# Keeping the whole triangle of a forward substitution in two PSUM banks, in a recurrence-and-experts kernel

## The chip, the cores and the metric

One Trainium2 core runs the kernel. The engines named here are TensorE (PE; its weight loads are PEld), VectorE (DVE), ScalarE (ACT), GpSimd (POOL) and SyncE (SP, which issues most transfers). The metric is the device time of one execution in microseconds (us), as the median over runs.

## What is computed

A recurrence with a 40x40 state over 768 steps, for 4 batches and 8 heads, followed by a layer of 8 experts. Cut to what matters:

```python
for t in range(S):                                   # S = 768, state [4,8,40,40]
    y[:, :, t] = einsum('bhd,bhde->bhe', rt, state)
    Sa = einsum('bhde,bhe->bhd', state, at)
    state = state*wt[:, :, None, :] - einsum('bhd,bhe->bhde', Sa, bt) \
            + einsum('bhd,bhe->bhde', vt, kt)
x = y.transpose(0, 2, 1, 3).reshape(B*S, H*D)        # 3072 tokens of 320
# for tokens whose x @ w_skip > 0: the expert of the largest gate logit,
out = xc + gate_w * (relu(xc @ w1[e]) @ w2[e])       # other tokens: out = x
```

## The kernel before

The 768 steps are cut into 24 chunks of 32 steps (`c`), four chunks to a phase (`ph`, `j` is the chunk in it). Inside a chunk the steps are coupled by a triangular 32x32 system per batch, head and chunk; its inverse is made ahead, for the four chunks of a phase at once. The chain from chunk to chunk is then matmuls alone: `rs` (state times r), `ux` (right-hand side), `uq` (times the inverse, read from `TB`), `sst` (new state), and `yy` (output, into `py`, multiplied by DVE into `XS`). Beside this chain each phase prepares the next one: scans of the decays on DVE (`scan_z`, `scan_w`), products on POOL (`kbm`, `l1a`, and the mask `R1t<-R1t,mc` behind each `uq`), the coupling matrices (`m1`: a PSUM tile that ACT copies and DVE transposes out), transposes (`kbt`, `wtt`), `m2`, and the routing of finished tokens (`route`: `xpose`, `score`, a rank `rk`).

The inverse itself is `tinv` (line 390): a forward substitution on DVE over the four chunks, 128 partitions wide. The coupling matrix `NLt` lies in SBUF (all tiles of that area appear as `M` in the trace). The triangle `X` is cut by columns. Columns 0 to 7 (`SPL=8`) lie in PSUM, in `X0`, which the trace calls `px`. Columns 8 to 31 lie in SBUF, in `Xi`. At step `i` group 0 handles row `j=i` of the PSUM part and group 1 row `j=i+8` of the SBUF part: a multiply of a column of `NLt` by a row of `X` into `tmp_`, and a subtraction of that from the rows below. Group 0 runs for 30 steps, group 1 for 22, so an inverse has 104 such instructions. In the trace group 0's are `M<-M,px` and `px<-px,M`; group 1's are both `M<-M`. At the end ACT copies `X0` into `Xi` (line 412) and DVE transposes the whole into `TB`. The first phase's inverse is made in another way (`tinv0`); `tinv` runs five times, for phases 1 to 5.

Eight PSUM banks of 512 floats are shared out at line 235: two `pq`, two `pc`, two `ps`, one `py` and one `px`. Chunks 0 and 1 and 22 and 23 are issued in the order in which the program is written, each ring of banks going round (`pq` serves `m1`, `kbt`, `wtt`, `m2` and routing). Chunks 2 to 21 are recorded and put in order by a planner (`Rec`, lines 58 to 210): it prices each instruction (line 93; a DVE `tensor_tensor` at 0.14 us + 1.05 ns per element, 1.6 times that slope where no operand is in PSUM), gives each PSUM tile a bank of `rec.banks` when its first instruction starts, whatever ring it was asked from, and keeps the two `ps` banks back for the state and for the oldest tile that waits. In its dependencies all `px` banks are one resource (line 90). What it emits is a fixed order for each engine. In the trace, L109 is what was issued directly and L209 what the planner emitted.

After the last chunk the banks are regrouped into three rings (line 767) for the experts (`experts`), whose matmuls end the kernel.

Of the kernel before, what the change touches and what calls it, by code (L numbers as in the profile page):

```python
# [8 lines left out]
F32 = mybir.dt.float32  # L9
I32 = mybir.dt.int32  # L10
AF = mybir.ActivationFunctionType
ALU = mybir.AluOpType
# [198 lines left out]
class Ring:  # L211
# [4 lines left out]
    def tile(s,shape,dt,tag=None,name=None):  # L216
# [4 lines left out]
        if len(shape)==2: return t  # L221
        ax=["abcd"[q] for q in range(len(shape)-1)]
        return t.rearrange("p ("+" ".join(ax)+") -> p "+" ".join(ax),**{a:v for a,v in zip(ax,shape[1:])})
G2=1; TD=(1,3); BU0=6; BU=(2,0,0,0); BX=(0,0,0,0,0,1,0,0,0,0,2,2,1,1,1,0,0,0,1,2,0,1,1,1,1,0,1,0,0); SPL=8; SCAN_POOL=0; RN=192; RB=((),()); RLAST=(('0c','1b','3a','3c'),('0a','0c')); P2=0
ROUTE=('0c',('0c','1b','3c'),('0c','1b','3c'))
WT=(1,0,0,0,1)
def attn(ctx,tc,i,m,out,X):
# [4 lines left out]
    cp=P("const",1).pool; wk=P("wk",1); wk2=P("wk2",2); wk3=P("wk3",3); wk4=P("wk4",4)  # L232
    pp=m.pp
    bk=lambda n,k: [pp.tile([128,512],F32,name=f"{n}{q}") for q in range(k)]
    PQ,PC,PS,PY,PX=bk("pq",2),bk("pc",2),bk("ps",2),bk("py",1),bk("px",1)
    rec.banks={t.name:t for t in PQ+PC+PS}; rec.rest=[t.name for t in PS]
    ps_c,ps_s,ps_p=(Ring(t,rec) for t in (PC,PS,PQ)); ps_y,ps_x=Ring(PY),Ring(PX); m.ps=ps_p
    V,A,G,TE,SP=nc.vector,nc.scalar,nc.gpsimd,nc.tensor,nc.sync
# [2 lines left out]
    NR1=2; NL=4; NL2=2; NTB=3  # L241
    mQ,idn=m.mQ,m.idn
    WR=m.WR
    mp=tc.tile_pool(name="M",bufs=1,side="right"); M=mp.__enter__().tile([128,13300],F32,name="M")
    off=[0]
    def mv(n):
        o=off[0]; off[0]+=n; return M[:,o:o+n]
    w_,Z_,rv,a_,AB_,NL_,X_,l3=(mv(n) for n in (1041,1042,1041,1024,1024,1024,1024,1024))
    AT_=[mv(256) for _ in range(2)]; Wx_=[mv(1040).rearrange("p (a b) -> p a b",a=16) for _ in range(4)]; tmp_=[mv(192) for _ in range(2)]; an=[0]
    sq=lambda t: t.rearrange("p (a b) -> p a b",a=32)  # L250
    KBa=[WR[:,2048*q:2048*q+2048].rearrange("p (u c q t) -> p u c q t",u=16,c=2,q=2) for q in range(4)]
    L1t=cp.tile([128,4096],F32,name="L1t")
# [80 lines left out]
    def m1(h,x,c,ev=None,late=None,FE=None):  # L333
# [11 lines left out]
        if c==0: an[0]+=1  # L345
        if c==0: AT[0]=AT_[an[0]%2].rearrange("p (h c t) -> p h c t",h=4,c=2) if h!=1 else SCR[:,1024+256*x:1280+256*x].rearrange("p (h c t) -> p h c t",h=4,c=2)
        at=AT[0]
# [42 lines left out]
    def tinv(ph):  # L390
        ab=AB[0]
        NLt=sq(NL_)
        V.transpose(NLt.rearrange("p a b -> p (a b)"),ab.rearrange("p a b -> p (a b)"))
        Xi=sq(X_)
        X0=ps_x.tile([128,32,SPL],F32)
        V.tensor_tensor(X0,NLt[:,0:SPL].rearrange("p s t -> p t s"),m.mT[:,:,0:SPL],ALU.mult)
        V.tensor_tensor(Xi[:,:,SPL:32],NLt[:,SPL:32].rearrange("p s t -> p t s"),m.mT[:,:,SPL:32],ALU.mult)
        V.memset(X0.rearrange("p a b -> p (a b)")[:,0:SPL*SPL:SPL+1],-1.0)
        V.memset(Xi.rearrange("p a b -> p (a b)")[:,33*SPL::33],-1.0)
        yield  # L400
        for i in range(1,31):
            q=[]
            for g,(j,lo,hi,X) in enumerate(((i,0,min(i,SPL),X0),(i+SPL,SPL,i+SPL,Xi))):
                if j>30: continue
                n=31-j; k=hi-lo
                tmp=tmp_[g]
                tv=tmp[:,:n*k].rearrange("p (a b) -> p a b",b=k)
                V.tensor_tensor(tv,NLt[:,j,j+1:32].unsqueeze(2).broadcast_to([128,n,k]),X[:,j,lo:hi].unsqueeze(1).broadcast_to([128,n,k]),ALU.mult)
                q.append((tv,X[:,j+1:32,lo:hi]))
            for tv,xv in q: V.tensor_tensor(xv,xv,tv,ALU.subtract)  # L410
            yield
        A.copy(Xi[:,:,0:SPL],X0)
        s0=(2*ph)%NTB; s1=(2*ph+1)%NTB
        t0=TBa[s0]; d=bass.AP(t0.tensor,t0.offset,(tuple(t0.ap[0]),(TBa[s1].offset-t0.offset,2),(32,16),(1,32)))
        V.transpose(d.rearrange("p h (x f) m -> p m x h f",x=2),Xi)
        yield
    def tinv0(Xi):
# [9 lines left out]
        for j in range(1,15):  # L427
            n=15-j; q=[]
            for g in range(G2):
                K=2//G2; k=slice(K*g,K*g+K)  # L430
                tv=tmp_[g][:,:K*n*j].rearrange("p (k a b) -> p k a b",k=K,b=j)
# [111 lines left out]
    def run_all(g):  # L543
        for _ in g: pass
    if 1:

        with tc.manual_schedule(engines={ET.Pool}):
# [4 lines left out]
            Xi=sq(X_)  # L552
# [46 lines left out]
            ps_p=Ring.of(pq.t+ps_y.t+ps_x.t)  # L599
# [20 lines left out]
            ps_p=r4  # L620
# [11 lines left out]
            ps_p=pq  # L632
# [17 lines left out]
        for c in range(NC):  # L650
            ph,j=divmod(c,4)
# [36 lines left out]
            if c==1: m1(3,1,0); m1(3,1,1); tg=tinv(1)  # L688
# [50 lines left out]
            if j==0 and c and ph+1<NPH: tg=tinv(ph+1)  # L739
# [24 lines left out]
        next(ra)  # L764
        yy(NC-1,1)
        run_all(ra)
        m.pr=[Ring.of(ps_c.t+ps_x.t),Ring.of(ps_s.t+ps_y.t),ps_p]
        p2=[m.pr[0].tile([128,512],F32) for _ in range(2)]; pt=[p2[0][:,0:256],p2[0][:,256:512],p2[1][:,0:256]]
        rb=m.route(xl[:,1:2],1,NC-1,lambda: onehot(1))
        warm(WT[1]); m.xacc(pt,0)  # L770
# [295 lines left out]
def build(tc,i,out):  # L1066
    with ExitStack() as ctx:
        cp=ctx.enter_context(tc.tile_pool(name="mcp",bufs=1))
        m=Moe(ctx,tc,i,out,cp)
        m.base1=cp.tile([128,8],F32,name="base1")  # L1070
        m.fi=cp.tile([1,3],I32,name="fi"); m.cw=cp.tile([128,24],F32,name="cw"); tc.nc.gpsimd.memset(m.cw,0.0)
        m.zc=cp.tile([128,1],F32,name="zc"); tc.nc.gpsimd.memset(m.zc,0.0)
        m.wc=cp.tile([128,1],F32,name="wc"); tc.nc.vector.memset(m.wc,-WMID)
        m.WR=cp.tile([128,11264],F32,name="WR"); m.raw=[m.WR[:,0:5632],m.WR[:,5632:11264]]
        P=lambda n,b,**k: tc.tile_pool(name=n,bufs=b,**k)
        with tc.manual_schedule(engines={ET.PE,ET.Activation,ET.DVE}), P("pp",1,space=PSUM) as m.pp, P("rt",1) as rt, P("xp",1) as xp:
            m.wk,m.xp=Static(rt,1),Static(xp,2)
            with ExitStack() as c2: attn(c2,tc,i,m,out,m.X)
            with P("mw2",2) as wk2, P("mw",1) as wk, P("mw4",4) as wk4: m.experts(wk,wk2,wk4,m.pr)
        general(m,m.fi,{q:i['raw_'+q] for q in 'rkvwab'},m.X)  # L1080
# [13 lines left out]
```

## Time and profile before

| what | value |
|---|---|
| median of 3 runs | 662.9 us (660.15 to 670.07) |
| the profiled execution's own time | 660.0 us |
| its span, first to last instruction | 658.2 us |
| mean granted TensorE clock | 0.88 |
| busy share of the span: PE, DVE, ACT, POOL | 77%, 79%, 64%, 49% |

The busy shares are means over stages with different limits. Three stages matter: the start and chunks 0 and 1 (to about 100 us), the planned chunks 2 to 21 (to about 480 us, in phases of some 80 us), and the last two chunks and the experts. How to read the rows below: "M<-M,px 128x120" is an instruction that writes a tile `M` of 128 partitions by 120 elements and reads `M` and `px`; "x44 | 26.7, 607 | 0.5" is 44 of them, 26.7 us busy in all, 607 ns each, and 0.5 us of idle time ahead of them.

### The profile page before, as it was taken

What the parts mean: (1) busy time and instruction counts of PE and PEld (TensorE: products, weight loads), DVE (VectorE), ACT (ScalarE), POOL (GpSimd) and SP (SyncE); (2) the same over time, 40 slices, a digit from 0 to 9 for tenths busy, and PEclk for the clock granted to TensorE, in tenths of its full rate; (3) what the DMA queues carried; (4) which work ended last, traced back from release to release, by engine and by line L of the source; (5) the groups of instructions that cost most, each with busy time, mean ns of one, the idle gap of its engine ahead of it and who ended that gap; (6) DMA issues with size and microseconds to landing.
All of it is one profiled execution on the core that took longest, in us unless ns stands there. A gap on an engine that the chain in (4) does not pass through costs nothing. (4 is left out here: it accounts for less than half of the span.)

```text
span 658.2 us, 30327 instructions
## 1 busy us (share of the span) xinstructions
PE 507.4 (77%) x13236; PEld 424.8 (65%) x13236; DVE 519.6 (79%) x1182; ACT 423.6 (64%) x1103; POOL 321.6 (49%) x256
## 2 busy tenths in 40 slices
PE   5766676687588778858758578888678799999994
PEld 2544465566476657637547466767566599899994
DVE  7998778988989789997998977884274458888871
ACT  6463565587766867757768578898966155455540
POOL 5491952645536665375733634333131156566661
PEclk9697778779877986888969799999977799999998
DMA  7784566352444525345334243454535166667200
GB/s 183 215 229 153 133 181 218 114 150 86 124 119 132 162 74 142 107 130 161 102 106 121 82 129 101 133 168 119 156 99 146 57 193 207 214 216 233 81 25 24
DMA packets 67817, 90.85 MB, mean 138 GB/s; under 512 B 32756, under 2 KB 54849, under 8 KB 66190
## 3 DMA queue, kind: packets, MB, share of 16 engines
q1 hardware_dynamic: 62638, 74.31, 39.0%
q0 software_dynamic: 5040, 14.54, 6.8%
q8 instruction: 106, 1.74, 1.1%
q14 instruction: 33, 0.27, 0.1%
HBM read 74.03 MB, written 17.08 MB: 138 GB/s over the span
## 5 line engine op out<-in xcount | busy, mean ns | idle before, releaser
L209 DVE TENSOR_TENSOR M<-M 128x130 f32<-128x130 f32 (+10 forms) x202 | 106.2, 526 | 2.2
L209 ACT COPY R1t<-pq 32x416 f32<-32x416 f32 (+4 forms) x218 | 84.1, 386 | 31.7 <-PE pq L209 28.7
L209 POOL TENSOR_TENSOR R1t<-R1t,mc 64x512 f32<-64x512 f32 x40 | 53.8, 1346 | 86.3 <-ACT R1t L209 62.8
L109 POOL TENSOR_TENSOR WL<-WR,WH 128x1280 fp32r<-128x1280 f32 (+1 forms) x21 | 57.6, 2779 | 8.7 <-ACT WH L109 8.6
L209 ACT COPY R1t<-pc 32x128 f32<-32x128 f32 (+4 forms) x146 | 53.3, 365 | 9.7 <-PE pc L209 7.7
L209 PE MATMUL py<-L2t,R1t 128*32 128x40 f32 x1280 | 22.9, 220 | 27.4 <-DVE XS L209 14.4
L209 POOL TENSOR_TENSOR WR<-WR,M 128x1024 f32<-128x1024 f32 x14 | 33.7, 2422 | 14.9 <-DMA WR<-kb 14.6
L109 ACT CAST WH<-WR 128x1024 fp32r<-128x1024 f32 (+1 forms) x35 | 39.6, 1132 | 0.0
L209 DVE TENSOR_TENSOR px<-px,M 128x168 f32<-128x168 f32 (+8 forms) x141 | 37.1, 263 | 3.1
L209 PEld LDWEIGHTS py<-L2t,R1t 128*32 128x32 f32 x1280 | 18.1, 124 | 31.9 <-issue 16.9
L109 DVE CAST ti<-xe 128x2 int32<-128x2 f32 x8 | 38.0, 4747 | 0.2
L109 POOL DMA_INDIRECT out<-ro,ti x16 | 15.7, 982 | 45.7 <-PE pq L109 21.8
L109 ACT ACTIVATE hH<-pc 128x512 fp32r<-128x512 f32 x21 | 12.6, 598 | 38.3 <-PE pc L109 38.3
L209 POOL DMA_INDIRECT xg<-XS,ix x20 | 24.6, 1232 | 25.1 <-DVE M L209 11.1
L209 DVE TENSOR_TENSOR M<-M,px 128x168 f32<-128x168 f32 (+8 forms) x141 | 34.7, 246 | 1.3
L209 DVE TENSOR_TENSOR_SCAN M<-M 128x1041 f32<-128x1041 f32 (+1 forms) x14 | 32.5, 2320 | 0.2
L209 POOL TENSOR_TENSOR M<-M,mc 128x256 f32<-128x256 f32 x16 | 12.1, 756 | 41.6 <-issue 25.4
L109 PE MATMUL pc<-xH,WH 128*128 128x256 f32 x126 | 32.4, 282 | 0.0
L109 DVE TENSOR_TENSOR WL<-WR,WH 128x1024 fp32r<-128x1024 f32 (+1 forms) x19 | 23.8, 1253 | 8.4 <-ACT WH L109 7.8
L209 DVE TENSOR_TENSOR R1t<-pc,D 40x512 f32<-40x512 f32 (+1 forms) x32 | 19.2, 601 | 13.3 <-PE pc L209 12.9
L209 PE MATMUL ps<-R1t,L2t 128*40 128x40 f32 (+1 forms) x512 | 26.3, 244 | 2.5 <-ACT R1t L209 1.1
L209 PE MATMUL pq<-UX,TB 32*32 32x72 f32 (+1 forms) x800 | 23.6, 262 | 5.5 <-ACT R1t L209 5.3
(380 smaller groups left out, 1692.9 us busy)
## 6 DMA issues: line engine op xcount, KB each, us to landing
WR<-kb SPq DMA_DIRECT2D x10, 1024.0 KB
WR<-w SPq DMA_DIRECT2D x16, 640.0 KB
WR<-w SPq DMA_DIRECT2D x16, 512.0 KB
vvt<-vv POOLq DMA_DIRECT2D x21, 256.0 KB, 4.1
rrt<-rr POOLq DMA_DIRECT2D x10, 512.0 KB, 5.6
M<-wt SPq DMA_DIRECT2D x9, 520.5 KB
M<-at SPq DMA_DIRECT2D x8, 512.0 KB
WR<-w SPq DMA_DIRECT2D x16, 256.0 KB
```

What stands on the lines that cost most here:

```text
L109: if not s.on: return fn(*a,**k)
L209: for fn,a,k,own in s.tasks[i].calls: fn(*[at(x,own) for x in a],**{n:at(x,own) for n,x in k.items()})
```

## The change

`X0` becomes 12 columns wide (`SPL=12`), and columns 12 to 31 go to a second PSUM tile `X1` of 20x20, which holds only the square that is not zero. To have a second `px` bank, one `pq` bank is given up. The planner then hands out five banks, and `pq` as a ring has one bank. Group 1 runs for 18 steps, so an inverse has 96 multiplies and subtractions. ACT copies two tiles into `Xi` at the end. The three rings of the experts keep their sizes, out of other banks.

```diff
-...; SPL=8; ...
+...; SPL=12; ...
-    PQ,PC,PS,PY,PX=bk("pq",2),bk("pc",2),bk("ps",2),bk("py",1),bk("px",1)
+    PQ,PC,PS,PY,PX=bk("pq",1),bk("pc",2),bk("ps",2),bk("py",1),bk("px",2)
-... M=mp.__enter__().tile([128,13300],F32,name="M")
+... M=mp.__enter__().tile([128,13400],F32,name="M")
-... tmp_=[mv(192) for _ in range(2)]; an=[0]
+... tmp_=[mv(240) for _ in range(2)]; an=[0]
-        Xi=sq(X_)
-        X0=ps_x.tile([128,32,SPL],F32)
+        Xi=sq(X_); K=32-SPL
+        X0=ps_x.tile([128,32,SPL],F32); X1=ps_x.tile([128,K,K],F32)
         V.tensor_tensor(X0,NLt[:,0:SPL].rearrange("p s t -> p t s"),m.mT[:,:,0:SPL],ALU.mult)
-        V.tensor_tensor(Xi[:,:,SPL:32],NLt[:,SPL:32].rearrange("p s t -> p t s"),m.mT[:,:,SPL:32],ALU.mult)
+        V.tensor_tensor(X1,NLt[:,SPL:32,SPL:32].rearrange("p s t -> p t s"),m.mT[:,SPL:32,SPL:32],ALU.mult)
         V.memset(X0.rearrange("p a b -> p (a b)")[:,0:SPL*SPL:SPL+1],-1.0)
-        V.memset(Xi.rearrange("p a b -> p (a b)")[:,33*SPL::33],-1.0)
+        V.memset(X1.rearrange("p a b -> p (a b)")[:,::K+1],-1.0)
         yield
         for i in range(1,31):
             q=[]
-            for g,(j,lo,hi,X) in enumerate(((i,0,min(i,SPL),X0),(i+SPL,SPL,i+SPL,Xi))):
+            for g,(j,o,X) in enumerate(((i,0,X0),(i+SPL,SPL,X1))):
                 if j>30: continue
-                n=31-j; k=hi-lo
-                tmp=tmp_[g]
-                tv=tmp[:,:n*k].rearrange("p (a b) -> p a b",b=k)
-                V.tensor_tensor(tv,NLt[:,j,j+1:32].unsqueeze(2).broadcast_to([128,n,k]),X[:,j,lo:hi].unsqueeze(1).broadcast_to([128,n,k]),ALU.mult)
-                q.append((tv,X[:,j+1:32,lo:hi]))
+                n=31-j; k=min(i,SPL) if g==0 else i
+                tv=tmp_[g][:,:n*k].rearrange("p (a b) -> p a b",b=k)
+                V.tensor_tensor(tv,NLt[:,j,j+1:32].unsqueeze(2).broadcast_to([128,n,k]),X[:,j-o,0:k].unsqueeze(1).broadcast_to([128,n,k]),ALU.mult)
+                q.append((tv,X[:,j+1-o:32-o,0:k]))
             for tv,xv in q: V.tensor_tensor(xv,xv,tv,ALU.subtract)
             yield
-        A.copy(Xi[:,:,0:SPL],X0)
+        A.copy(Xi[:,:,0:SPL],X0); A.copy(Xi[:,SPL:32,SPL:32],X1)
...
-        m.pr=[Ring.of(ps_c.t+ps_x.t),Ring.of(ps_s.t+ps_y.t),ps_p]
+        m.pr=[Ring.of(PC+PX[:1]),Ring.of(PS+PX[1:]),Ring.of(PQ+PY)]
```

## Rows read from the trace of the kernel before

**Rows 1.** The page's first part: busy us, share of the span, instructions of each engine.

```profile
PE 507.4 (77%) x13236; PEld 424.8 (65%) x13236; DVE 519.6 (79%) x1182; ACT 423.6 (64%) x1103; POOL 321.6 (49%) x256
```

**Rows 2.** Busy time by stretch: start:end, length, then engines, PEclk, DMA share, GB/s.

```profile
89.00:136.60 47.60, 33.16 (x1169) 28.02 (x1166) 41.77 (x132) 31.32 (x88) 19.47 (x17) 0.79 0.44 134
...
158.50:220.30 61.80, 46.01 (x1468) 37.71 (x1468) 57.84 (x153) 44.50 (x128) 31.84 (x27) 0.81 0.41 121
...
383.60:444.50 60.90, 50.73 (x1830) 41.34 (x1834) 47.64 (x174) 51.69 (x150) 19.06 (x20) 0.97 0.47 131
444.50:475.00 30.50, 25.11 (x890) 20.12 (x878) 11.02 (x35) 27.31 (x80) 8.09 (x8) 1.00 0.46 134
...
sum 247.00, PE 180.36 PEld 149.72 DVE 222.91 ACT 179.52 POOL 135.09; mean PE 60.12 PEld 49.91 DVE 74.31 ACT 59.84 POOL 45.03
```

**Rows 3.** Timeline of DVE: end of one inverse (TB), start of the next (M).

```profile
136.60 1.99 DVE L209 STREAM_TRANSPOSE TB<-M 128x1024 f32<-128x1024 f32 x1 [0.84 <-ACT M L209]
...
158.53 1.22 DVE L209 STREAM_TRANSPOSE M<-M 128x1024 f32<-128x1024 f32 x1
```

**Rows 4.** Groups of group-1 instructions, stretches from 89.0, from 136.6, from 383.6.

```profile
L209 DVE TENSOR_TENSOR M<-M 128x130 f32<-128x130 f32 (+10 forms) x26 | 10.0, 385 | 0.2
...
L209 DVE TENSOR_TENSOR M<-M 128x22 f32<-128x22 f32 (+10 forms) x44 | 26.7, 607 | 0.5
...
L209 DVE TENSOR_TENSOR M<-M 128x22 f32<-128x22 f32 (+10 forms) x44 | 14.4, 328 | 0.4
```

**Rows 5.** Instructions of tile px in the planned part: ns minimum/median/maximum, first and last start.

```profile
L209 DVE TENSOR_TENSOR M<-M,px x141: 131/240/345, 101.8 to 442.8; 128x168 f32<-128x168 f32 x9, 128x160 f32<-128x160 f32 x5, 128x152 f32<-128x152 f32 x5, 128x144 f32<-128x144 f32 x5
L209 DVE TENSOR_TENSOR px<-px,M x141: 161/267/357, 102.2 to 443.0; 128x168 f32<-128x168 f32 x9, 128x160 f32<-128x160 f32 x5, 128x152 f32<-128x152 f32 x5, 128x144 f32<-128x144 f32 x5
```

**Rows 6.** Timeline of POOL and DVE, 113 to 121 us: start, us, engine.

```profile
114.01 2.45 POOL L209 TENSOR_TENSOR R1t<-R1t,mc 64x512 f32<-64x512 f32 x1 [9.00 <-ACT R1t L209]
116.54 4.27 POOL L209 TENSOR_TENSOR WR<-WR,M 128x1024 f32<-128x1024 f32 x2
...
115.32 0.25 DVE L209 TENSOR_TENSOR M<-M,px 128x120 f32<-128x120 f32 x1
115.49 1.11 DVE L209 TENSOR_TENSOR M<-M 128x120 f32<-128x120 f32 x1
...
116.72 2.02 DVE L209 TENSOR_SCALAR D<-M 128x16 f32<-128x16 f32 x1
```

**Rows 7.** Groups with shapes kept apart: count, busy us, mean ns of one.

```profile
L209 DVE TENSOR_TENSOR M<-M,mc 128x768 f32<-128x768 f32 x4 | 6.0, 1498 | 0.0
...
L209 DVE TENSOR_TENSOR M<-M 128x130 f32<-128x130 f32 x20 | 5.8, 290 | 0.3
...
L209 DVE TENSOR_TENSOR px<-M,mc 128x256 f32<-128x256 f32 x4 | 3.3, 827 | 0.1
...
L209 DVE TENSOR_TENSOR px<-px,M 128x130 f32<-128x130 f32 x4 | 1.2, 301 | 0.1
...
L209 ACT COPY M<-px 128x256 f32<-128x256 f32 x5 | 1.9, 372 | 0.1
```

**Rows 8.** Timeline: a uq tile in its bank, filled by PE, emptied by ACT.

```profile
191.19 0.92 PE L209 MATMUL pq<-UX,TB 32*32 32x104 f32 x32
...
192.47 2.02 ACT L209 COPY R1t<-pq 32x416 f32<-32x416 f32 x4
```

**Rows 9.** Timeline, chunk 1: two m1 tiles in the two pq banks.

```profile
82.54 1.07 PE L109 MATMUL pq<-WR,L1t 128*32 128x64 f32 x64
...
83.24 0.88 ACT L109 COPY M<-pq 128x128 f32<-128x128 f32 x2
...
83.71 0.76 DVE L109 STREAM_TRANSPOSE M<-pq 128x128 f32<-128x128 f32 x2 [6.19 <-POOL WR L109]
```

**Rows 10.** Timeline, chunk 23: score behind m2, and the uq that follows.

```profile
495.71 0.62 PE L109 MATMUL pq<-wg,xT 128*32 128x9 f32 x24
495.88 1.06 ACT L109 COPY R1t<-pq 32x128 f32<-32x128 f32 x4
...
496.26 1.61 PE L109 MATMUL pc<-UX,TB 32*32 32x104 f32 x32
```

More of the change, by code (lines that the diff above doesn't have):

```diff
@@ L223, in tile @@
         return t.rearrange("p ("+" ".join(ax)+") -> p "+" ".join(ax),**{a:v for a,v in zip(ax,shape[1:])})
-G2=1; TD=(1,3); BU0=6; BU=(2,0,0,0); BX=(0,0,0,0,0,1,0,0,0,0,2,2,1,1,1,0,0,0,1,2,0,1,1,1,1,0,1,0,0); SPL=8; SCAN_POOL=0; RN=192; RB=((),()); RLAST=(('0c','1b','3a','3c'),('0a','0c')); P2=0
+G2=1; TD=(1,3); BU0=6; BU=(2,0,0,0); BX=(0,0,0,0,0,1,0,0,0,0,2,2,1,1,1,0,0,0,1,2,0,1,1,1,1,0,1,0,0); SPL=12; SCAN_POOL=0; RN=192; RB=((),()); RLAST=(('0c','1b','3a','3c'),('0a','0c')); P2=0
 ROUTE=('0c',('0c','1b','3c'),('0c','1b','3c'))
@@ L243, in attn @@
     WR=m.WR
-    mp=tc.tile_pool(name="M",bufs=1,side="right"); M=mp.__enter__().tile([128,13300],F32,name="M")
+    mp=tc.tile_pool(name="M",bufs=1,side="right"); M=mp.__enter__().tile([128,13400],F32,name="M")
     off=[0]
@@ L248, in attn @@
     w_,Z_,rv,a_,AB_,NL_,X_,l3=(mv(n) for n in (1041,1042,1041,1024,1024,1024,1024,1024))
-    AT_=[mv(256) for _ in range(2)]; Wx_=[mv(1040).rearrange("p (a b) -> p a b",a=16) for _ in range(4)]; tmp_=[mv(192) for _ in range(2)]; an=[0]
+    AT_=[mv(256) for _ in range(2)]; Wx_=[mv(1040).rearrange("p (a b) -> p a b",a=16) for _ in range(4)]; tmp_=[mv(240) for _ in range(2)]; an=[0]
     sq=lambda t: t.rearrange("p (a b) -> p a b",a=32)
```

## The prediction, made before the changed kernel was run

> **What bounds the kernel now.** I read the page's busy shares first, then the busy time by stretch, then the groups of instructions inside one stretch, then single stretches of the timeline. The shares of the whole span [rows 1] say little: DVE has 79%, PE 77%. So the planned part is cut at the transposes that finish an inverse into `TB`. There are five of them, the first at 136.6 us [rows 3], the others at 220.3, 300.6, 383.6 and 444.5 us, the bounds of my stretches. In the three full stages between 136.6 and 383.6 us (247.0 us together, 82.3 us each) DVE is busy 222.9 us, 90%; ACT has 59.8 us a stage (73%), PE 60.1 (73%) [rows 2]. Inside a stage, the stretch in which the inverse is made, from 158.5 us [rows 3] to its end, has DVE at 57.84 of 61.8 us, 94% [rows 2]. DVE sets the pace there. In the next stage, from 383.6 us, where nothing is prepared for a seventh phase, four chunks go through in 60.9 us with ACT at 51.69 us (85%) and DVE at 78%; after that comes a stretch with ACT at 27.31 of 30.5 us (90%) [rows 2]. So when DVE is not the limit, the chunk chain and ACT are, with ACT 85 to 90% busy.
>
> Now what DVE's time is made of. The 44 group-1 instructions of an inverse take 26.7 us in the first full stage, 607 ns each [rows 4]; the other two full stages look alike, within 2 us. The group-0 instructions, the same operation with one operand in PSUM, take 240 and 267 ns in the median and never more than 357 ns, in 282 of them [rows 5]. The sizes are alike: an inverse's group 1 has 2,024 products in 22 multiplies, 92 each, and its group 0 2,936 in 30, 98 each. So size does not explain 607 ns. The timeline does: while POOL works from 114.01 us on, a group-0 multiply takes 0.25 us as always, and the group-1 multiply of the same 120 elements right behind it takes 1.11 us and ends with the POOL instruction [rows 6]. Without POOL, group 1's largest forms average 290 ns [rows 7]. What an SBUF-only instruction pays is a wait for POOL, and it is paid on the engine that is the limit.
>
> **The change, part by part.** *Group 1 goes to PSUM.* I price it by the group-0 rows, 0.25 us each [rows 5]. The wait that goes is 44 x (0.607 - 0.25) = 15.7 us in a full stage, 26 x (0.385 - 0.25) = 3.5 us in the stretch from 89 us, and 44 x (0.328 - 0.25) = 3.4 us in the stage from 383.6 us [rows 4]. Eight instructions fewer take off 8 x 0.25 = 2 us. Against it, group 0 runs alone for 12 steps at the end and not 8, with each instruction waiting for the one before; other work of DVE can stand between them, so I book 1 us of the 2 us.
>
> [...] Group 1's 130-element form costs 290 ns in SBUF, and group 0's of the same size 301 ns [rows 7], so moving an instruction costs about 10 ns, 36 x 0.01 = 0.4 us an inverse. [...]
>
> *The start of an inverse.* Two multiplies, 256 elements into PSUM at 0.83 us and 768 at 1.50 us [rows 7], become 384 and 400 elements into PSUM. By the first row that is 2.5 us, by the second 1.5; against 2.3 us I count nothing.
>
> *The end.* ACT copies 384 and 400 elements in place of 256 at 0.37 us [rows 7]: at most 0.37 x 784/256 = 1.1 us, so +0.8 us for ACT, between the last subtraction and `TB`.
>
> *What a full stage then takes.* DVE needs 74.3 - 15.7 - 1 = 57.6 us. ACT needs 59.8 + 0.8 = 60.6 us, now the larger. At ACT's 85% a stage lasts 71.3 us; at 90% 67.7 us; if nothing followed DVE's gain, 82.3 us. I take 85%, because that stage has the same chain of four chunks. PE's 60.1 us is at a granted clock of about 0.8 (0.81 in the stretch from 158.5 us), and the stage that ran faster was granted 0.97 [rows 2], so PE is no earlier limit.
>
> *One bank less for the planner.* The program asks for 74 tiles in four chunks (4 `rs`, 8 `ux`, 8 `uq`, 8 `m1`, 8 `kbt`, 4 `wtt`, 8 `m2`, 10 of the routing, 16 `sst`). A `uq` tile is held from 191.19 to 194.49 us, 3.3 us [rows 8]. If all are held so long that is 244 us of bank time: 49% of six banks over 82.3 us, but 69% of five over 71.3 us. There is room, but bursts will wait. Lower bound nothing, since `m1` and `rs` tiles wait for DVE today and will be freed sooner; upper bound 16 us a stage, the whole gain. No row shows a plan with five banks; I take 2.7 us, in the lower part because the banks have room on average. A stage then lasts 74 us: 3 x (82.3 - 74) = 25 us gained. The planner also prices group 1 lower and takes both `px` banks as one resource; DVE is one queue, so I count nothing for either.
>
> *One `pq` bank where the order is written.* In chunk 1 thirteen tiles (`m1`, `kbt`, `wtt`, `m2`, one `s2`) go through `pq`. Now two `m1` are filled back to back, and both leave by 84.47 us [rows 9]. With one bank the second fill (half of 1.07 us) waits for the first transpose, and each pair ends about 1 us later. PE's queue stands meanwhile, with the chain behind it. Six pairs at 1 us give 6 us; PE is busy only 33.16 of 47.6 us there [rows 2], which hides some. Bounds 0 and 12 us, I take 3 us, which meets the 3.5 us that DVE gets back in the same stretch (88% busy, 3 us of it counted). In chunks 22 and 23 a `score` is filled at 495.71 us while `m2` is still being copied out until 496.94 us [rows 10]: it will wait 1.2 us, and the `uq` at 496.26 us is behind it on PE. A second such place follows from the code in chunk 22. I book 2 us, between 0 and 3. The stage from 383.6 us gets 0: ACT sets it, and what DVE gets back the banks take.
>
> **The sum.** 660.0 us (the profiled execution) - 25 - 3 + 3 + 0 + 2 = 637 us. That execution is 2.9 us under the median of the runs; I put the median at 638 us.
>
> **Rivals.** *A, all of it comes back:* no bank ever waits and ACT reaches 90%. A stage takes 67.7 us, 3 x 14.6 = 44 us, and 660 - 44 - 3 + 1 = 614 us. For it: the second stretch of 90% [rows 2], and a plan that was bound by DVE's waits, which it does not price. Against it: ACT has never been that busy over a whole stage.
>
> *B, the banks take the gain:* from 0.15 us of waiting per tile (74 x 0.15 = 11 us) a stage is back at 82 us, and the kernel at 660 to 665 us. For it: bank use goes from 49 to 69%, and more than half of it lies on three banks that every kind of tile may take. Against it: the order is planned for five banks.
>
> *C, slower:* the same wait, but on the chain. PE's queue is in order, so a `ux` that waits for a bank holds the `sst` behind it, and ACT's copies then come late, which hold the banks longer. From 15.4/74 = 0.21 us per tile the kernel is over 2% slower (11 us of gain and 13.3/3 us of loss in a stage); at 0.25 us a stage is 89.8 us and the kernel 684 us. Against it: today's holds have more than one tile's length of slack on average.
>
> *D, the waits move and do not go:* DVE still has instructions that wait for POOL, such as the `TENSOR_SCALAR` of 16 elements that took 2.02 us at 116.72 us [rows 6], and the group-1 instruction that waited in their place no longer shields them. POOL is busy 45 of 82.3 us [rows 2], so if two thirds of the 15.7 us reappear on scans, routing and copies, a stage gains 5 us at most, less 2.7 us for the banks: 653 us. Against it: no group-0 instruction, 282 of them, was ever held [rows 5], and the others are few beside 44. [...]
>
> **How the numbers follow.** The forecast, 626 to 650 us, 0.46. A, 0.16. B, 0.16. C, 0.14. D, 0.08. About 2% (13 us) is what a measurement of this kernel can tell from no change. Forecast and A are faster by more: 0.62; B and D are within: 0.24; C slower: 0.14. The range, 614 to 662 us, takes in A's middle, the forecast and D, and about half of B, and leaves out C.
>
> **What would show it.** The changed profile should have `px<-px,M` and `M<-M,px` alone in the substitution, 96 to an inverse, none above 0.4 us; DVE's busy time down by some 16 us a full stage, to about 70 to 78%; the `TB` transposes some 74 us apart; ACT over 80% in each stage. If DVE falls but the stages stay at 82 us, it is B, with PE or its weight loads waiting on ACT or DVE for a `pq`, `pc` or `ps` bank. If `SCAN`, `COPY` and `TENSOR_SCALAR` grow by 10 us a stage, it is D. Chunk 1 should end later against its own start. What makes the prediction wrong most easily is the price of the fifth bank, which no row shows.

## The result, and the profile after

The changed kernel takes 653.0 us as the median of three runs (652.0 to 654.0), beside 664.0 us for the kernel before in the same comparison. The ratio, which here and below is taken over undisturbed runs alone (one of 752.4 us is left out here) and so is not the quotient of the medians, is 0.9884, 95% interval 0.9834 to 0.9933. It is 1.2% faster: the interval leaves out 1, but this is within the 2% that count as no change. I had forecast 638 us. The profiled execution of the changed kernel took 653.0 us, so 7 us came out of 660.0 where the sum said 23.

The page of after, first part (columns as in [rows 1]):

```profile
PE 504.5 (77%) x13236; PEld 416.4 (64%) x13236; DVE 455.5 (70%) x1142; ACT 426.1 (65%) x1108; POOL 325.1 (50%) x256
```

DVE lost 64 us of busy time against [rows 1]. The instructions of tile px in the planned part of after (minimum/median/maximum ns) answer to [rows 5]:

```profile
L209 DVE TENSOR_TENSOR M<-M,px x222: 140/240/383, 103.3 to 425.2; 128x168 f32<-128x168 f32 x9, 128x210 f32<-128x210 f32 x5, 128x220 f32<-128x220 f32 x5, 128x228 f32<-128x228 f32 x5
L209 DVE TENSOR_TENSOR px<-px,M x222: 161/250/399, 103.8 to 425.4; 128x168 f32<-128x168 f32 x9, 128x210 f32<-128x210 f32 x5, 128x220 f32<-128x220 f32 x5, 128x228 f32<-128x228 f32 x5
...
L209 DVE TENSOR_TENSOR px<-M,mc x8: 814/829/853, 162.1 to 388.9; 128x384 f32<-128x384 f32 x4, 128x400 f32<-128x400 f32 x4
```

All 444 multiplies and subtractions are at the price of group 0, and the longest is 399 ns: the wait for POOL is gone from the substitution. The `TB` transposes come at 143.4, 218.3, 289.0, 360.9 and 439.4 us. Busy time of after between them (columns as in [rows 2]), the last line the sum and mean of the first three stages:

```profile
143.45:218.30 74.85, 51.96 (x1850) 41.44 (x1840) 59.09 (x175) 56.75 (x160) 43.73 (x34) 0.91 0.44 130
218.30:289.00 70.70, 54.10 (x1834) 43.90 (x1832) 55.10 (x177) 53.53 (x155) 38.78 (x35) 0.86 0.45 134
289.00:360.90 71.90, 52.66 (x1931) 42.69 (x1929) 52.17 (x171) 55.10 (x160) 43.15 (x37) 0.93 0.39 119
360.90:439.40 78.50, 60.47 (x2251) 49.10 (x2239) 46.14 (x183) 64.93 (x186) 27.81 (x27) 0.98 0.46 130
...
sum 217.45, PE 158.72 PEld 128.03 DVE 166.35 ACT 165.38 POOL 125.66; mean PE 52.91 PEld 42.68 DVE 55.45 ACT 55.13 POOL 41.89
```

The three full stages take 217.45 us where they took 247.0 [rows 2]: 29.5 us gained, 4.5 more than forecast. But the stage that follows takes 78.5 us in place of 60.9, and the first `TB` is 6.85 us late: 29.5 - 17.6 - 6.85 = 5.1 us is all that the last `TB` is earlier. What the inverses won was handed back at once, because the chunks did not follow. That shows in when a `TB` is used. Two inverses of before (each `TB` transpose on DVE, then the first `uq` on PE that reads it; columns as in [rows 6]):

```profile
220.32 1.98 DVE L209 STREAM_TRANSPOSE TB<-M 128x1024 f32<-128x1024 f32 x1
231.21 0.92 PE L209 MATMUL pq<-UX,TB 32*32 32x104 f32 x32
...
383.61 1.98 DVE L209 STREAM_TRANSPOSE TB<-M 128x1024 f32<-128x1024 f32 x1
391.80 0.92 PE L209 MATMUL pc<-UX,TB 32*32 32x104 f32 x32
```

and the same two of after:

```profile
218.27 2.01 DVE L209 STREAM_TRANSPOSE TB<-M 128x1024 f32<-128x1024 f32 x1
235.44 0.92 PE L209 MATMUL pq<-UX,TB 32*32 32x104 f32 x32
...
360.86 2.00 DVE L209 STREAM_TRANSPOSE TB<-M 128x1024 f32<-128x1024 f32 x1
386.77 0.92 PE L209 MATMUL pc<-UX,TB 32*32 32x104 f32 x32
```

Before, the transpose of the inverse for chunk 16 began 8.2 us ahead of its use; after, 25.9 us ahead. It came 22.8 us earlier and was used 5.0 us earlier. So the pace is to be read from the chunks. From the first `uq` of chunk 4 to that of chunk 16, three phases, busy time of before, and of after:

```profile
152.20:391.80 239.60, 174.12 (x5942) 144.34 (x5937) 216.53 (x548) 172.99 (x496) 129.62 (x110) 0.84 0.41 120
```

```profile
158.20:386.80 228.60, 165.93 (x5936) 133.84 (x5937) 166.92 (x528) 173.76 (x498) 130.57 (x110) 0.91 0.42 124
```

DVE gave up 49.6 us there and the chunks 11.0 us: a phase of four chunks takes 76.2 us in place of 79.9. After, no engine is over 76% (ACT); DVE and PE are at 73%. The 7.0 us of the two profiled executions are then: 6.0 us lost up to chunk 4 (its `uq` at 158.2 in place of 152.2), 11.0 gained to chunk 16, 1.3 lost to chunk 20, 1.3 gained to chunk 23, 2.0 gained behind it.

What held the last `TB` in the stage from 360.9 us is not the substitution. DVE and ACT of after:

```profile
425.39 0.18 DVE L209 TENSOR_TENSOR px<-px,M 128x12 f32<-128x12 f32 x1
...
432.63 0.17 DVE L209 TENSOR_REDUCE mx<-sc 128x2 f32<-128x16 f32 x1 [6.99 <-ACT sc L209]
...
439.37 1.92 DVE L209 STREAM_TRANSPOSE TB<-M 128x1024 f32<-128x1024 f32 x1
```

```profile
435.08 0.49 ACT L209 COPY M<-px 128x384 f32<-128x384 f32 x1
...
438.45 0.48 ACT L209 COPY M<-px 128x400 f32<-128x400 f32 x1
```

The substitution ended at 425.6 us, DVE stood idle for 6.99 us, and ACT, which empties the chunk's tiles in a planned order, came to the two `px` tiles at 435.08 and 438.45 us. Nobody needed this `TB` before 450.9 us.

### The profile page after: what moved, and what is told of

Its sections match the earlier page's. It is cut to its first block, busy times and chain, and to the rows that moved or that the text cites. A ratio compares the mean times of both kernels' runs of the same rounds, so it can differ in the third digit from the quotient of the medians.

```text
span 651.2 us, 30293 instructions
## 1 busy us (share of the span) xinstructions
PE 504.5 (77%) x13236; PEld 416.4 (64%) x13236; DVE 455.5 (70%) x1142; ACT 426.1 (65%) x1108; POOL 325.1 (50%) x256
## 3 DMA queue, kind: packets, MB, share of 16 engines
q8 instruction: 106, 1.74, 1.1%
## 5 line engine op out<-in xcount | busy, mean ns | idle before, releaser
L209 ACT COPY R1t<-pc 32x128 f32<-32x128 f32 (+4 forms) x228 | 85.3, 374 | 25.4 <-PE pc L209 18.8
L209 POOL TENSOR_TENSOR R1t<-R1t,mc 64x512 f32<-64x512 f32 x40 | 59.0, 1474 | 80.6 <-ACT R1t L209 55.5
L109 POOL TENSOR_TENSOR WL<-WR,WH 128x1280 fp32r<-128x1280 f32 (+1 forms) x21 | 57.6, 2773 | 8.7 <-ACT WH L109 8.6
L209 DVE TENSOR_TENSOR px<-px,M 128x210 f32<-128x210 f32 (+11 forms) x222 | 53.7, 269 | 2.1
L209 DVE TENSOR_TENSOR M<-M,px 128x210 f32<-128x210 f32 (+11 forms) x222 | 51.1, 257 | 1.9
L209 ACT COPY R1t<-pq 32x256 f32<-32x256 f32 (+4 forms) x114 | 43.9, 385 | 9.9 <-PE pq L209 8.3
L209 DVE TENSOR_TENSOR R1t<-pc,D 40x512 f32<-40x512 f32 (+1 forms) x42 | 26.5, 630 | 14.6 <-PE pc L209 14.0
L209 PE MATMUL py<-L2t,R1t 128*32 128x40 f32 x1280 | 22.8, 216 | 13.7 <-POOL R1t L209 7.3
L209 PE MATMUL ps<-R1t,L2t 128*40 128x72 f32 (+1 forms) x560 | 28.4, 242 | 6.2 <-ACT R1t L209 4.3
L209 PEld LDWEIGHTS ps<-R1t,L2t 128*40 128x40 f32 x560 | 21.3, 131 | 11.5 <-ACT R1t L209 5.9
L109 PE MATMUL ps<-mc 128*128 128x512 f32 x36 | 24.2, 780 | 4.7 <-DMA mc<-mc 3.5
L209 POOL DMA_DIRECT2D vvt<-vv x20 | 11.7, 586 | 32.2 <-PE pc L209 16.4
```

Of the source, the lines that this page charges most:

```text
L109: if not s.on: return fn(*a,**k)
L209: for fn,a,k,own in s.tasks[i].calls: fn(*[at(x,own) for x in a],**{n:at(x,own) for n,x in k.items()})
```

## Experiments

Times are medians; each ratio is to the kernel before on the same chip, with its 95% interval. "Chunk 4 to 20" is the time between their first `uq` in the profile: 302.4 us before, 292.6 after. DVE's busy time, where it is given for a whole kernel, is that of the profiled execution, and stands beside that execution's own time.

### What the waits are worth, in a fixed order

Two kernels keep the order of every engine as it was (in the traces too, but for neighbouring short instructions) and change only how long DVE's instructions take. The first is after with `X1` in SBUF again; the planner is told to treat that area as `px`, in its dependencies and in its prices.

```diff
+    x1=1<<30; mn=None
+    def as_px(s,ap): return ap.name==s.mn and s.x1<=ap.offset%ap.ap[0][0]<s.x1+400
...
+        if s.as_px(ap):
+            q,m=s.mask(ap); return [(('px',),q,m>>s.x1)]
...
-        X0=ps_x.tile([128,32,SPL],F32); X1=ps_x.tile([128,K,K],F32)
+        X0=ps_x.tile([128,32,SPL],F32); ps_x.tile([128,K,K],F32); X1=X1s
```

> The changed kernel with its 20x20 group put back into SBUF while the planner still prices and orders it as PSUM: the order of every engine is the changed kernel's, only 36 instructions an inverse read two SBUF operands again and wait for POOL. So the difference to the changed kernel is what DVE's waits alone are worth in that order. Theory 'DVE's waits set the pace' (the prediction's step): 10 to 15 us more busy DVE a stage lengthen it by as much, 675 to 690 us. Theory 'chain' (the inverse is ready 20 us early and the chunks wait for other things): 653 to 660 us, with the transposes into TB later and the uq of the chunks where they were.

Measured: 660.54 us, 0.9996 [0.9958, 1.0033]. The page's first part and groups of this kernel (columns as in [rows 1] and [rows 4]):

```profile
PE 502.1 (76%) x13236; PEld 419.3 (64%) x13236; DVE 485.2 (74%) x1142; ACT 426.6 (65%) x1108; POOL 319.2 (48%) x256
...
L213 DVE TENSOR_TENSOR M<-M 128x88 f32<-128x88 f32 (+8 forms) x162 | 60.4, 373 | 0.2
L213 DVE TENSOR_TENSOR px<-px,M 128x108 f32<-128x108 f32 (+8 forms) x141 | 41.3, 293 | 2.0
L213 DVE TENSOR_TENSOR M<-M,px 128x108 f32<-128x108 f32 (+8 forms) x141 | 39.5, 280 | 1.8
```

These are 141 us, against 222 x 0.269 + 222 x 0.257 = 117 us for the same 444 instructions of after: 24 us of waits come back (DVE's busy time goes from 455.5 to 485.2 us) and cost 7 us, chunk 4 to 20 going from 292.6 to 301.4 us. Taking DVE's waits away is thus worth all that the change gained, but in this order only 0.3 us for each us of wait. The row says one thing more: in after's order group 1 waits 162 x (0.373 - 0.25) = 20 us, in before's 202 x (0.526 - 0.25) = 56 us. The other order hides 36 us by itself, and this kernel, which also has the change's five banks, single `pq` ring and one resource for two `px` banks, is no faster than before.

The second keeps before's order and puts group 1's products into the free half of the `px` bank, so that its subtractions have one operand in PSUM. The planner is told to treat that half as the SBUF scratch tile (not printed):

```diff
-        X0=ps_x.tile([128,32,SPL],F32)
+        xb=ps_x.tile([128,512],F32); X0=xb[:,0:32*SPL].rearrange("p (a b) -> p a b",b=SPL); xt=xb[:,32*SPL:]
...
-                tmp=tmp_[g]
+                tmp=xt if g else tmp_[g]
```

> The kernel before in exactly its order, with the products of group 1 written to the free half of its px bank: its 22 subtractions an inverse then read one SBUF operand and not two, and about half of DVE's waits for POOL go; nothing else moves. Theory 'DVE's waits set the pace': about half of 25 us comes back, 645 to 650 us. Theory 'chain': 657 to 664 us.

Measured: 662.63 us, 1.0053 [1.0008, 1.0097]. Groups of before:

```profile
L209 DVE TENSOR_TENSOR M<-M 128x130 f32<-128x130 f32 (+10 forms) x202 | 106.2, 526 | 2.2
L209 DVE TENSOR_TENSOR px<-px,M 128x168 f32<-128x168 f32 (+8 forms) x141 | 37.1, 263 | 3.1
L209 DVE TENSOR_TENSOR M<-M,px 128x168 f32<-128x168 f32 (+8 forms) x141 | 34.7, 246 | 1.3
L209 DVE TENSOR_TENSOR_SCAN M<-M 128x1041 f32<-128x1041 f32 (+1 forms) x14 | 32.5, 2320 | 0.2
...
L209 DVE COPY XS<-mc 128x2 f32<-128x2 f32 x10 | 3.5, 353 | 0.0
L209 DVE TENSOR_SCALAR ix<-sl 128x2 int32<-128x2 f32 x10 | 3.4, 340 | 0.3
```

and of this kernel:

```profile
L212 DVE TENSOR_TENSOR px<-M 128x130 f32<-128x130 f32 (+10 forms) x101 | 57.3, 567 | 3.1
L212 DVE TENSOR_TENSOR M<-M,px 128x132 f32<-128x132 f32 (+16 forms) x242 | 54.0, 248 | 4.6
L212 DVE TENSOR_TENSOR px<-px,M 128x168 f32<-128x168 f32 (+8 forms) x141 | 37.3, 264 | 4.3
L212 DVE TENSOR_TENSOR_SCAN M<-M 128x1041 f32<-128x1041 f32 (+1 forms) x14 | 36.0, 2573 | 0.2
...
L212 DVE COPY XS<-mc 128x2 f32<-128x2 f32 x10 | 8.8, 879 | 0.0
...
L212 DVE TENSOR_SCALAR ix<-sl 128x2 int32<-128x2 f32 x10 | 7.1, 712 | 0.3
```

The substitution's instructions add up to 23 us less (178 against 57.3 + 242 x 0.248 + 37.3 = 155 us). Of that 5.3 us reappear on ten two-element copies, 3.7 on ten `TENSOR_SCALAR` and 3.5 on the scans: 12.5 us, over half, moved, as rival D had it. The rest did not free DVE either. The page's first part, and busy time from chunk 4 to 16, of this kernel:

```profile
PE 502.4 (76%) x13236; PEld 418.6 (63%) x13236; DVE 523.2 (79%) x1182; ACT 424.3 (64%) x1103; POOL 321.0 (49%) x256
...
153.40:394.40 241.00, 167.83 (x5951) 138.42 (x5938) 216.22 (x548) 173.46 (x496) 129.30 (x110) 0.87 0.41 119
```

DVE is busy for 523.2 us where it was 519.6 [rows 1], and from chunk 4 to 16 for 216.2 us where it was 216.5: what is left of the 23 us went where the records of neighbouring instructions overlap less. From 100 to 480 us DVE's durations add up to 351.2 us in before and 339.9 here, and the busy time, in which an overlap counts once, is 314.7 and 317.2 us. So this kernel takes waits off the substitution and nothing off DVE, and it cannot say what DVE's time is worth in before's order. It says something on PE, which was busy 167.8 us in place of 174.1 from chunk 4 to 16, at a granted clock of 0.87 in place of 0.84: the chunks were no faster for it.

### How much of the triangle has to be in PSUM

Sixteen columns in the one `px` bank, sixteen in SBUF, six banks by need as before:

```diff
-...; SPL=8; ...
+...; SPL=16; ...
...
-... tmp_=[mv(192) for _ in range(2)]; an=[0]
+... tmp_=[mv(240) for _ in range(2)]; an=[0]
```

> The kernel before with 16 columns in its one px bank, all 512 floats of it, and 16 in SBUF; six banks as before. SBUF-only instructions fall from 44 to 28 an inverse. Theory 'banks' (DVE's waits were the limit, and only the lost bank hid the gain): about two fifths of 16 us a stage come back with nothing lost, 645 to 652 us. Theory 'chain': the inverse is ready earlier and the chunks don't follow, 658 to 664 us.

Measured: 637.48 us, 0.9643 [0.9568, 0.9718], below both ranges, chunk 4 to 20 in 286.1 us: three times the gain of the change, without its second bank. Its instructions in SBUF still wait:

```profile
L209 DVE TENSOR_TENSOR M<-M 128x50 f32<-128x50 f32 (+6 forms) x122 | 53.5, 439 | 1.3
```

At 0.25 us each these would be 30 us, so 23 us of waiting is left.

Thirteen columns and group 1's products in the rest of the `px` bank leave 17 multiplies of an inverse with both operands in SBUF:

```diff
-...; SPL=8; ...
+...; SPL=13; ...
...
-        X0=ps_x.tile([128,32,SPL],F32)
+        xb=ps_x.tile([128,512],F32); X0=xb[:,0:32*SPL].rearrange("p (a b) -> p a b",b=SPL); xt=xb[:,32*SPL:]
...
-                tmp=tmp_[g]
+                tmp=xt if g else tmp_[g]
```

> Six planned banks, 13 columns in the one px bank, and the products of the SBUF group written into what is left of that bank, so that a subtraction reads one operand from SBUF and not two: only its 17 multiplies an inverse still read two SBUF operands, against 28 instructions with 16 columns and 44 before. Theory 'DVE's waits for POOL': the subtractions cost 0.25 us without outliers, DVE is busy some 2 us a stage less than with 16 columns, and the time is 632 to 638 us. If what counts is the number of SBUF instructions in any form (34 here): 638 to 645 us.

Measured: 648.43 us, 0.9804 [0.9742, 0.9867], above both ranges. The substitution waits less than with sixteen columns (its 76 planned multiplies of that kind took 441 ns each, 14.5 us over 0.25 us each, beside 23 us), but DVE as a whole is busier. The page's first part for thirteen columns, for sixteen in the other order of the next section, and for sixteen:

```profile
PE 504.2 (78%) x13236; PEld 419.3 (65%) x13236; DVE 503.9 (78%) x1132; ACT 424.7 (66%) x1103; POOL 324.9 (50%) x256
...
PE 501.1 (78%) x13236; PEld 418.3 (65%) x13236; DVE 497.4 (77%) x1102; ACT 423.6 (66%) x1103; POOL 320.4 (50%) x256
...
PE 500.0 (79%) x13236; PEld 417.6 (66%) x13236; DVE 487.5 (77%) x1102; ACT 423.8 (67%) x1103; POOL 317.0 (50%) x256
```

The profiled executions took 648.5, 645.4 and 638.7 us. With before (519.6 and 660.0 us) and the kernel above (523.2 and 662.3 us) these are five kernels with six planned banks and one `px` bank, and over them 36 us of DVE's busy time go with 24 us of time: 0.66 for one. The orders differ, so this is what goes together and not a price in a fixed order; before in the other order of the next section (516.9 and 655.5 us) lies 3 us under the line.

### What any other order is worth

The planner's price of a hand-over between engines, `HOP`, is raised a little. This changes no work, only the order. In before, in after, and in the kernel with sixteen columns:

```diff
-    HOP=0.12; PW=1.25
+    HOP=0.13; PW=1.25
```

> The kernel before, with the planner's assumed delay between engines at 0.13 us in place of 0.12: the same work, another order in chunks 2 to 21. It measures what an arbitrary change of the order is worth. Theory 'order is a lottery': it differs from 661 us by 5 us or more, either way. Theory 'order is steady': 658 to 664 us.

> The changed kernel with the same shift of the planner's assumed delay (0.13 us). Theory 'lottery': 5 us or more away from 653.5 us, either way. Theory 'steady, and the one px resource holds it back': 650 to 656 us.

> 16 columns in one px bank, six planned banks, and the planner's assumed delay at 0.13 us: the same work in another order. If the 637.5 us are the design's: 633 to 642 us. If they were a lucky order: 645 us or more.

Measured: 656.23 us, 1.0007 [0.9964, 1.005]; 649.11 us, 0.9887 [0.9798, 0.9976]; 643.25 us, 0.9711 [0.9612, 0.9811]. So another order of the same work moved the ratio by nothing in two kernels and by 0.7% in the third (against 0.9643, not resolved by the intervals). The 1.1% of after stands in both orders, and so does the lead of sixteen columns.

### What the fifth bank costs

Before, with only five banks handed out by the planner; the rings of the written order stay:

```diff
-        bank={}; at={k:0.0 for k in s.banks}; last={}
+        bank={}; at={k:0.0 for k in s.banks if k!=s.held}; last={}
...
-    rec.banks={t.name:t for t in PQ+PC+PS}; rec.rest=[t.name for t in PS]
+    rec.banks={t.name:t for t in PQ+PC+PS}; rec.rest=[t.name for t in PS]; rec.held=PQ[1].name
```

> The kernel before, with one pq bank held back from the planner alone: chunks 2 to 21 are planned with five banks, the chunks in written order keep two pq banks, and the inverse stays half in SBUF. Theory 'banks' (the missing bank costs in the planned part what DVE got back, some 8 us in each of three full stages and the next): 680 to 695 us, with the uq of chunk 4 to that of chunk 16 taking 260 us or more where before took 240. Theory 'chain' (the chain of chunks was not waiting for DVE's inverse in the first place, and a bank more or less does not matter): 658 to 668 us.

Measured: 655.95 us, 0.9945 [0.9909, 0.9981], chunk 4 to 20 in 295.9 us. The bank costs nothing visible here. The same edit on top of sixteen columns, in both orders:

> The kernel with 16 columns in one px bank (637.5 us) with one pq bank held back from the planner, nothing else. Theory 'banks only when DVE is relieved' (a fifth bank costs nothing while DVE's waits set the pace, as the kernel before with five planned banks showed, but costs once they are fewer): 645 to 650 us. Theory 'no price' (five banks are enough, and the changed kernel loses by its dependencies and its order): 634 to 641 us.

> 16 columns in one px bank with five planned banks (652 us), with the planner's assumed delay at 0.13 us. If the fifth bank's price of 14.6 us is real: 648 to 656 us. If it was an unlucky order: below 645 us.

Measured: 652.07 us, 0.9894 [0.9854, 0.9934], above both ranges, and 647.98 us, 0.9796 [0.9733, 0.9858]. Against 0.9643 and 0.9711, going from six banks to five costs 2.5% in the one order and 0.85% in the other, where the intervals overlap. So it has a price in the first order; in the second that is not resolved.

### What one resource for two `px` banks costs

After, with the two `px` banks kept apart in the planner's dependencies (line 90), in both orders:

```diff
-        if n[:2] in ('py','px'): n=(n[:2],)
+        if n[:2] in ('py','px'): n=(n[:2],n)
```

> The changed kernel with the two px banks as two resources in the planner's dependencies, so that the two groups of the substitution are two chains and not one of 96 instructions, with a lower priority. Theory 'priority' (the doubled chain pushed the inverse ahead of the chunk chain in the plan): 640 to 648 us. Otherwise as the changed kernel, 650 to 657 us.

> The changed kernel with the two px banks as two resources (646.3 us) and the same shift of the planner's assumed delay. Theory 'one px resource costs 7 us': 643 to 649 us, again below its twin with one resource. Theory 'lottery': anywhere between 640 and 656 us, and not below its twin by more than a few us.

Measured: 646.31 us, 0.978 [0.9696, 0.9863], and 643.81 us, 0.9773 [0.9695, 0.9851]. Against 0.9884 and 0.9887, 1.1% each time. The intervals of each pair overlap a little, and the reading rests on both orders giving the same. How the merged name costs this is argued from the code and not shown: with one resource the two groups of a step can stand one behind the other in the planner's dependencies, and it ranks an instruction by the length of the work behind it, so that a longer chain of the substitution rises above the chunks' own work.

### The written order with one `pq` bank

After, with a second bank for the `pq` ring in chunks 0, 1, 22 and 23, and the first inverse in the old way (`tinv1`, a copy of the old `tinv`):

```diff
-            ps_p=pq
+            ps_p=m.ps=Ring.of(PQ+PX[1:])
...
-            if c==2: rec.on=True
+            if c==2: rec.on=True; ps_p=m.ps=Ring(PQ,rec)
...
-            if c==1: m1(3,1,0); m1(3,1,1); tg=tinv(1)
+            if c==1: m1(3,1,0); m1(3,1,1); tg=tinv1(1)
```

> The changed kernel with two banks again for the pq ring in chunks 0 and 1 and in 22 and 23: the second px bank serves there, and the first of the five inverses is made as in the kernel before. The planned part has five banks and both groups in PSUM from the second inverse on. Theory 'written order' (one pq bank costs some 5 us in chunks 0 and 1, where the uq of chunk 4 came 6 us later than before, and 1 to 2 us at the end): 645 to 648 us, the first transpose into TB at 137 us in place of 143. If the five-bank plan alone sets the time: 651 to 655 us.

Measured: 651.87 us, 0.9848 [0.9763, 0.9933]. The first `uq` of chunk 2 comes at 109.3 us, as before (110.2), and not at 116.9 as after; chunk 4 at 152.7, not 158.2. Then chunk 4 to 20 takes 297.2 us in place of 292.6, and little of it is left at the end (the ratio is not resolved from 0.9884). The delay by the ring is shown; that it costs the kernel as much is not.

### Better uses of the eight banks

Seven banks by need, `px` among them, with the dependencies kept apart; first on after, then on sixteen columns:

```diff
-        if n[:2] in ('py','px'): n=(n[:2],n)
+        if n[:2] in ('py','px') and n not in s.banks: n=(n[:2],)
...
-    rec.banks={t.name:t for t in PQ+PC+PS}; rec.rest=[t.name for t in PS]
-    ps_c,ps_s,ps_p=(Ring(t,rec) for t in (PC,PS,PQ)); ps_y,ps_x=Ring(PY),Ring(PX); m.ps=ps_p
+    rec.banks={t.name:t for t in PQ+PC+PS+PX}; rec.rest=[t.name for t in PS]
+    ps_c,ps_s,ps_p=(Ring(t,rec) for t in (PC,PS,PQ)); ps_y,ps_x=Ring(PY),Ring(PX,rec); m.ps=ps_p
```

> The changed kernel with the two px banks in the planner's pool too: seven banks, of which an inverse holds two while it is being made, and any tile may take them in between (in the changed kernel from the copy-out of one inverse to the start of the next, 24 to 26 of some 75 us). The two px banks are two resources in it. Theory 'banks' (five are too few once DVE is relieved): 632 to 641 us, below the 646 us of the changed kernel with separate resources. Theory 'banks are not it': 643 to 650 us.

> 16 columns in one px bank (637.5 us with six planned banks), with that px bank in the planner's pool as well, seven in all. Theory 'banks': the step from five to six was worth 14.6 us here; a seventh for a third of the time gives a few more, 630 to 636 us. Theory 'six are enough': 635 to 641 us.

Measured: 641.27 us, 0.9716 [0.9651, 0.9781], and 639.36 us, 0.9648 [0.9563, 0.9732]. With sixteen columns it brings nothing over six banks.

The substitution put back by 15 us in the planner's ranking, on the kernel with `px` kept apart, on seven by need (with the test for `px` through the tile's own name), and on sixteen columns:

```diff
-        s.key=[i*w-s.FAR*t.up for i,t in enumerate(s.tasks)]
+        s.key=[i*w-s.FAR*t.up+(15.0 if t.e=='V' and any(n[0]=='px' for n,q,m in t.W+t.R) else 0.0) for i,t in enumerate(s.tasks)]
```

> The changed kernel with two px resources (646.3 us), and in the planner's priorities every instruction of the substitution put back by 15 us against the rest. Theory 'priority' (the inverse is made too early, 20 us before its first use, and takes DVE from the chain's evacuations): 636 to 643 us. Theory 'the chain waits for banks, not for DVE': 643 to 650 us. If the inverse becomes late instead: 655 us or more.

> Both groups in PSUM, seven banks handed out by need, and the substitution put back by 15 us in the planner's priorities. If priority and banks add up (6 us from the demotion and 5 us from the banks, each seen alone on the changed kernel with two px resources at 646 us): 632 to 638 us. If they are two ways to the same slack: 638 to 643 us.

> 16 columns in one px bank, six planned banks (637.5 and 643 us in two orders), with the same demotion of the instructions on px. If priority helps there too: 630 to 635 us. If the inverse has no more slack to give, since its SBUF instructions still wait for POOL: 637 to 646 us.

Measured: 640.44 us, 0.9702 [0.9653, 0.975]; 624.65 us, 0.9437 [0.9358, 0.9516]; 636.98 us, 0.96 [0.9525, 0.9676]. The first and third are not resolved from the kernels that they start from (0.978 and 0.9643). The second is, below both ranges: 0.9437 against 0.9716, the fastest kernel here, 5.6% under before (626.9 us in the profiled execution, with DVE busy 472.4 us). Its stretch from chunk 4 to chunk 16:

```profile
153.80:365.60 211.80, 167.41 (x5946) 136.85 (x5942) 178.92 (x528) 174.04 (x498) 124.68 (x110) 0.91 0.46 136
```

It is 16.8 us shorter than after's, with the same work on ACT (174.04 against 173.76 us) and PE (167.41 against 165.93, at the same granted clock of 0.91), and with more on DVE (178.92 against 166.92, 84% of the stretch). So a DVE at 84% goes with faster chunks than a DVE at 73%: what it does first, and the banks, matter more than how busy it is. Without the lower rank the seven banks give this for the same stretch:

```profile
155.60:373.90 218.30, 166.69 (x5940) 136.91 (x5936) 181.55 (x527) 174.58 (x498) 126.56 (x110) 0.92 0.44 131
```

The rank alone thus takes 6.5 us off it.

## Why the prediction was wrong, point by point

**The pace, and what a full stage then takes: this is the step that failed.** I took the spacing of the `TB` transposes [rows 3] for the pace of the chunks, 82.3 us a stage, and let it come down to 74 us. From first `uq` to first `uq`, chunk 4 to 16, a phase took 79.9 us before and 76.2 us after. So 3 x (82.3 - 79.9) = 7 of the forecast 25 us were not there to win: in before the inverses fell back against the chunks, from 15.6 us ahead of their first reader to 8.2, and I never read that time. The other 7 of the 14 us that are missing are 3 x (76.2 - 74): with DVE relieved, ACT did not come to hold the chunks at 85%. It reached 76%, and something else held them. Part of it is the one resource for both `px` banks, below: with the two kept apart a phase took 75.3 and 72.6 us in the two orders, in place of 76.2 and 74.9.

**DVE as the limit of the kernel before** is not refuted by this. Over the five kernels with six banks the time goes with DVE's busy time at 0.66 for one, and my sum had 11 us of stage time for 16.7 us off DVE, 0.66 too. An inverse that is ready early does not free the chunks from DVE, since their own products (`R1t<-pq,D`) stand in DVE's one order between the substitution's instructions. Followed back through the trace, each step to what released it, from the first `uq` of chunk 16 to that of chunk 4, before spends 150 of 240 us on DVE and after 96 of 229, with 48 on ACT where it was 20; this is a reading, since releasers are inferred. In the changed kernel DVE's waits count for less: 24 us of them given back in its own order cost 7 us, 0.3 for one.

**The granted clock** rose from 0.84 to 0.91 from chunk 4 to 16, and PE was busy 8.2 us less. That it made the 11.0 us is unlikely: in before's order 6.3 us less of PE brought nothing, and the fastest kernel is 16.8 us shorter at the same 0.91.

**Group 1 at 0.25 us** was right: medians of 240 and 250 ns, none above 399. DVE's need of 57.6 us a stage came out at 55.45. The substitution's instructions that read two operands in SBUF took 373 to 567 ns in the mean in the kernels that have them, and those with one operand in PSUM 246 to 269 ns in before and after.

**The start of an inverse:** its two multiplies cost 0.83 us each, 1.7 us together, inside the bounds of 1.5 and 2.5 us, where 2.3 us had gone before. **The end** was mis-sized: the two copies take 0.97 us of ACT as forecast (0.49 + 0.48), but they stand in ACT's order, and the last `TB` came 14 us behind the last subtraction.

**A full stage** was forecast at 74 us by ACT at 85%; the `TB` transposes are 72.5 us apart on average, a hit, but of the wrong thing. My own mark for rival B, stages still at 82 us, was to be read from the same transposes, so it could not have told.

**One bank less**, 2.7 us a stage, was of the right size where DVE had been relieved: 0.85% and 2.5% of 660 us are 5.6 and 16.5 us, over the five planned phases 1.1 to 3.3 us each (only the larger is clear of noise). It is nothing in before's order. **One resource for both `px` banks**, counted at nothing because "DVE is one queue", costs 1.1%, 7 us, as far as two orders tell: the planner's order changes, whatever DVE's queue does. That is the second step that failed. Together, what the change gives up weighs more than I booked: at like busy time of DVE (485.2 and 487.5 us) the changed kernel with `X1` in SBUF took 660.4 us and sixteen columns on six banks 638.7, some 22 us apart.

**One `pq` bank in the written order** was booked at 3 us, met by DVE's gain. Chunk 2 came 6.7 us later and chunk 4 6.0 us: inside my bounds of 0 to 12, twice the value taken, and the gain of DVE did not meet it. **The stage from 383.6 us** at nothing: chunk 16 to 20 lost 1.3 us. **The tail** at 2 us lost was not seen: chunk 20 to 23 took 46.3 us in place of 47.6.

So of the 16 us between the sum and the profile, 14 are the three stages and 6 the start; the end gave back some 4. **Rivals:** C is refuted by the time itself, 653 us; A would have needed ACT at 90%; D held in before's order, where taking 23 us off the substitution left DVE as busy as it was, but not in after, where DVE's busy time fell by 64 us and the same copies and `TENSOR_SCALAR` grew by 1.6 us each and the scans by 2.7; B's size of time was near, 653 against 660, but its cause is at most a part.

**What stays open.** What a us of DVE's time is worth in before's own order: the kernel made for it freed none. How the 22 us divide among the fifth bank, the merged name and the single `pq` bank. Which resource sets the chunks' pace in after: no engine is above 76% and no single wait dominates. Whether the columns in PSUM add anything to the fastest kernel beside eight in before's manner, since a kernel with eight columns and the lower rank was not run.

## What to carry to other kernels

The spacing of results that are made ahead is not the pace of those who use them: read the time from each result to its first reader, and take the pace from the readers (here 79.9 us a phase, and not 82.3). To price a kind of wait, put it back with every queue in the same order, where 24 us of waits were worth 7 us here; and see that the engine's busy time moved at all, which it did not when 23 us were taken off one kind of instruction. And where a planner hands out order and buffers, ask of every edit what it does to dependencies and ranks: a merged name cost some 1.1%, and seven shared banks with background work ranked lower run 4.5% under the changed kernel at the same work.

## What the runs showed of the hardware

A wait for POOL that was taken off some DVE instructions fell on others of two elements: ten copies went from 353 to 879 ns each when 101 subtractions in the same order stopped waiting, and ten `TENSOR_SCALAR` from 340 to 712 ns. They read one tile each. In before the three of them that took over 0.5 us (1.74, 0.57 and 1.87 us) end 0.02 to 0.03 us behind the end of a POOL instruction. With group 1's products in the `px` bank one copy took 5.39 us; a POOL instruction began while it ran, and it ends 0.03 us behind that one:

```profile
370.43 5.39 DVE L212 COPY XS<-mc 128x2 f32<-128x2 f32 x1
...
373.64 2.15 POOL L212 TENSOR_TENSOR L1t<-M 64x1024 f32<-64x1024 f32 x1
```

The scans of 1,041 elements went from 2,320 to 2,573 ns in the same kernel. On the other side, POOL's mask `R1t<-R1t,mc` took 1,346 ns in before and 1,474 in after (40 of them, the same shape), so freeing DVE did not make POOL faster.
